# Reordering the last recurrence steps of a fused attention and MLP kernel, and storing the second product's result block by block

## The chip, the core and the metric

The kernel runs on one core of a Trainium2 chip. A core has five engines that work side by side, each with its own instruction queue that it takes in order: TensorE (matmuls, "PE" in the profile, with its weight loads shown as "PEld"), VectorE ("DVE"), ScalarE ("ACT"), GpSimd ("POOL") and SyncE ("SP"). Data comes from and goes to device memory by DMA; in this kernel SP and POOL issue all of these transfers. Matmuls write to PSUM, which has eight banks of 128 x 512 float32 values here; the other engines copy results from there to SBUF.

The metric is the device time of one execution, in microseconds. Smaller is better.

## The reference: what is computed

The first stage is a linear recurrence for each of 4 x 8 batch and head pairs, over 768 tokens with a state of 40 x 40; the second stage is a two-layer network with a Mish activation on the 3072 tokens that result.

```python
def _attn_ref(r, k, v, w, a, b):
    B, H, S, D = r.shape            # 4, 8, 768, 40
    state = np.zeros((B, H, D, D), dtype=np.float32)
    y = np.zeros_like(r)
    for t in range(S):
        ...
        y[:, :, t] = np.einsum('bhd,bhde->bhe', rt, state)
        Sa = np.einsum('bhde,bhe->bhd', state, at)
        state_decay = state * wt[:, :, None, :] - np.einsum('bhd,bhe->bhde', Sa, bt)
        state = state_decay + np.einsum('bhd,bhe->bhde', vt, kt)
    return y

def _moe_ref(x, w_in, w_out):       # x: 3072 x 320, w_in: 320 x 2048, w_out: 2048 x 320
    h = x @ w_in
    sp = np.where(h > 20.0, h, np.log1p(np.exp(np.minimum(h, 20.0))))
    g = h * np.tanh(sp)
    return g @ w_out
```

## The kernel before

**The recurrence.** The 768 tokens are cut into 12 chunks of 64 (`nch` = 12, `C` = 64). A chunk's update is written in closed form, which needs the inverse of a small triangular matrix for each chunk and head. The work on one chunk falls into parts:

- `pre_a` (L126) loads a chunk's inputs (SP queue) and forms its scaled operands. It does not depend on the state.
- `pre_inv` (L205) inverts the triangular blocks of a pair of chunks by forward substitution: a long dependent chain of small VectorE operations (L214, L216), closed by two transposes (L218, L220). There are six pairs, numbered 0 to 5.
- `post_inv` (L223) is the merge of a pair: from the inverted halves it builds the full inverse and from that the operand `KT` of both chunks. For each chunk of the pair it runs two sets of small matmuls (L232, L241) with a ScalarE copy between them (L235), copies pieces into `bdT` on ScalarE (L249 to L251), multiplies (L258) and copies the result into `KT` on ScalarE (L260). The merge of pair 5 serves steps 10 and 11.
- `step` (L349) carries the state through chunk c. It has five parts for each of two groups g of heads, issued in the order of `SORD`: `step_a` (L273: copies the state into `VS`, multiplies with `KT`, L284, and negates the result into `UVT`, L286), `step_u` (L288: transposes, L293, and copies, L294), `step_d` (L296: transposes the state, L304, and copies it, L305), `step_b` (L308: matmuls, L314, and a masked copy on VectorE, L316) and `step_c` (L319: matmuls, L334 and L339, then the new state on VectorE, L342 and L346, and the output `yev` on ScalarE, L343). At its end it issues the loads of the next step (`step_loads`, L265) and the stores of its own y (L370), all on the POOL queue. Each step needs the state of the one before.

The y of every step goes to a buffer in device memory, from which the second stage reads it.

**The dense stage.** `Mlp.run` (L550) works on 6 blocks of 512 tokens. `load_x` (L558) loads a block's y and a scale on the SP queue, multiplies them on VectorE (L567) and splits the product into a high part (L568) and a low rest (L569, L570). `mlp1` (L573), called for q = 0 to 7 in each block, forms 2 x 128 of the 2048 hidden columns: 16 matmuls (L584), Mish on ScalarE (L586), and a split into a high part `gh` (L589) and a rest `gl` (L590). `mlp2` (L595), which follows `mlp1` by three calls, adds the q-th share of the second product: 24 matmuls of 320 columns (L604 to L606) into four PSUM tiles `po`, one for each 128 tokens. At q = 7 the four are copied to SBUF tiles `os` by ScalarE (L610) and stored by SP (L611).

The weights arrive as 64-bit values and are converted on the chip: `load_f32` (L445) loads a chunk on the SP queue (L453), and ScalarE and VectorE turn it into float32 (L459 to L463); `split` (L489) then makes a high part (L494) and a rest (L495). `first` (L527) converts what is left of w_in once the `pre_a` buffers are free; `second` (L532) converts three chunks of w_out and opens the buffers of the dense stage that reuse room of the merge; `third` (L545) converts the other five.

**What sets the order.** The program is written as straight-line Python. A scheduler walks it at compile time and fixes the order of each engine's queue: it takes an instruction by its place in the program, as soon as what it needs is there by the scheduler's own reckoning. The helper `at(tc, k)` (L44) moves all that is issued inside it forward by `OFF[k]` places (backward if the number is negative); two nested calls move by both. In the main loop (L392 on) the end of the program stands in this order: step 8; the inversion and the merge of pair 5 (`inv(5)`, keys I5, I and J5); `first` (key W, 600); step 9; `second` (key V, 400); step 10; step 11; and then the dense stage. In a step every part has a key of its own besides the step's (`c0` 600, `u1` 250, `d0` 250, `d1` 150).

Of the kernel before, what the change touches and what calls it, by code (L numbers as in the profile page):

```python
# [7 lines left out]
F32 = mybir.dt.float32  # L8
# [28 lines left out]

OFF = {'I': 80, 'T1': 80, 'P00': -40, 'P10': 80, 'P11': 40, 'b0': 15, 'c0': 600, 'u0': -15, 'u1': 250, 'd0': 250,
       'd1': 150, 'W': 600, 'V': 400, 'E': 150, 'I0': 600, 'I1': 300, 'I2': 300, 'I3': 300, 'I4': 300, 'p4': 15,
       'I5': 300, 'J5': 600, 's0': 150, 's2': -15, 's3': 80, 's4': 250, 's6': -15, 's7': -40, 's8': 150, 's10': -150}  # L40
SORD = 'a0 b0 u0 d0 a1 b1 u1 d1 c0 c1'


# [423 lines left out]
def load_yp(nc, i, yD, pD, y, p, dup):  # L467
    ys = yD[i].rearrange("b e a (g t) -> (b e a g) t", g=2)
    ps = pD[i].rearrange("b e a (g s t) -> (b e a g) s t", g=2, t=65)[:, :, 0:64]
    p = p.rearrange("p k (s t) -> p k s t", t=64)  # L470
    for k in range(2):
        nc.sync.dma_start(out=y[:, k], in_=ys[k * 128:k * 128 + 128])
        nc.sync.dma_start(out=p[:, k], in_=ps[k * 128:k * 128 + 128])
    for k in range(2 if dup else 1):
        nc.sync.dma_start(out=y[k * 64:k * 64 + 64, 2], in_=ys[256:320])
        nc.sync.dma_start(out=p[k * 64:k * 64 + 64, 2], in_=ps[256:320])


class Mlp:
# [70 lines left out]
    def run(self, nsc):  # L550
        tc, nc, W, yD, pD, out = self.tc, self.tc.nc, self, self.yD, self.pD, self.out
        V, A, PE, SP, G = nc.vector, nc.scalar, nc.tensor, nc.sync, nc.gpsimd
        T = 512
        ps_h, mpa = self.ps_h, self.mpa
        mp = self.pool("mp", 2, "left")
        ps_o = self.pool("ps_o", 8 - NH, "left", space=PSUM)

        def load_x(i):  # L558
            y = self.mpx.tile([128, 3, T], F32, name="xy", bufs=NXP)
            p = self.mpx.tile([128, 3, T], F32, name="xp", bufs=NXP)  # L560
            for c in range(2):
                t = slice(c * 256, c * 256 + 256)
                load_yp(nc, 2 * i + c, yD, pD, y[:, :, t], p[:, :, t], True)

            xh = self.mpx.tile([128, 3, T], F32R, name="xh", bufs=NX)
            xl = self.mpx.tile([128, 2, T], F32R, name="xl", bufs=NX)
            V.tensor_tensor(out=y, in0=y, in1=p, op=ALU.mult)  # L567
            A.copy(xh, y)  # L568
            V.tensor_tensor(out=xl, in0=y[:, 0:2], in1=xh[:, 0:2].bitcast(F32), op=ALU.subtract)  # L569
            V.tensor_tensor(out=xh[64:128, 2], in0=y[64:128, 2], in1=xh[64:128, 2].bitcast(F32), op=ALU.subtract)  # L570
            return xh, xl

        def mlp1(q, xh, xl):  # L573

            g = mpa.tile([128, 2, T], F32, name="g", bufs=NHB)
            for j in range(2):
                ph = ps_h.tile([128, T], F32, name="ph")
                f = slice((q % 2 * 2 + j) * 128, (q % 2 * 2 + j) * 128 + 128)
                h, l = W.ih[q // 2], W.il[q // 2]

                for n, (w, x) in enumerate(((h[:, 0, f], xh[:, 0]), (h[:, 0, f], xl[:, 0]), (h[:, 1, f], xh[:, 1]),
                                            (h[:, 1, f], xl[:, 1]), (l[:, 0, f], xh[:, 0]), (l[:, 1, f], xh[:, 1]),
                                            (h[:, 2, f], xh[:, 2]), (l[:, 2, f], xh[:, 2]))):
                    PE.matmul(ph, w, x, start=(n == 0), stop=(n == 7), skip_group_check=True)  # L584

                A.activation(g[:, j], ph, AF.Mish)  # L586
            gh = mp.tile([128, 2, T], F32R, name="gh", bufs=NGB)
            gl = mp.tile([128, 2, T], F32R, name="gl", bufs=NGB)
            A.copy(gh, g)  # L589
            V.tensor_tensor(out=gl, in0=g, in1=gh.bitcast(F32), op=ALU.subtract)  # L590
            return gh, gl

        pos = {}

        def mlp2(i, q, gh, gl):  # L595
            if q == 0:
                pos[i] = [ps_o.tile([128, 320], F32, name="po") for _ in range(4)]
            po = pos[i]
            for j in range(2):
                f = q * 2 + j  # L600
                oh, ol = (w[f // 2][:, f % 2 * 320:f % 2 * 320 + 320] for w in (W.oh, W.ol))
                for k in range(4):
                    t = slice(k * 128, k * 128 + 128)
                    PE.matmul(po[k], gh[:, j, t], oh, start=(f == 0), stop=False, skip_group_check=True)  # L604
                    PE.matmul(po[k], gh[:, j, t], ol, start=False, stop=False, skip_group_check=True)  # L605
                    PE.matmul(po[k], gl[:, j, t], oh, start=False, stop=(f == 15), skip_group_check=True)  # L606
            if q == 7:
                for k in range(4):
                    o = mp.tile([128, 320], F32, name="os")
                    A.copy(o, po[k])  # L610
                    SP.dma_start(out=out[i * T + k * 128:i * T + k * 128 + 128], in_=o)  # L611

        wait = []
        x = load_x(0)
        for i in range(nsc // 2):
            for q in range(8):
                wait.append((i, q) + mlp1(q, *x))
                if (i, q) == (0, 0):
                    self.third()
                if q == 3 and i + 1 < nsc // 2:  # L620
                    nx = load_x(i + 1)
                if len(wait) > LAG:
                    mlp2(*wait.pop(0))
            x = nx
        for w in wait:
            mlp2(*w)
# [32 lines left out]
```

## Time and profile before

| | |
|---|---|
| three executions | 826.63, 828.1, 833.62 us (median 828.1) |
| the profiled execution | 823.92 us, of which the span from the first to the last instruction is 821.8 us |
| mean granted TensorE clock in it | 0.953 |
| TensorE busy | 722.7 us (88%) |
| VectorE busy | 458.7 us (56%) |
| ScalarE busy | 428.7 us (52%) |
| GpSimd busy | 103.4 us (13%) |
| read from and written to device memory | 48.79 MB and 11.86 MB |

How to read it: times inside the profile count from the first instruction. "L258" is line 258 of the kernel; `pa<-bdT,HA` means that the tile `pa` is written from `bdT` and `HA`; what stands in square brackets is the time for which the engine was idle just before, and what ended that. A busy TensorE is not one at its peak, since matmuls are pipelined: what counts is the distance from one matmul's start to the next. In the first 100 us TensorE is busy for only 51.18 us, while the first chunks are prepared. From there to 460 us the recurrence runs, with the inversions on VectorE beside it; after that comes the dense stage.

### The profile page before, as it was taken

How to read it: one execution, taken by the hardware profiler on the slowest of the kernel's cores; microseconds unless marked ns; L12 is line 12 of the kernel's file. 1: busy time of each engine (PE TensorE's matmuls, PEld its weight loads, DVE VectorE, ACT ScalarE, POOL GpSimd, SP SyncE). 2: the span in 40 equal slices, each digit the busy share in tenths (PEclk: the TensorE clock that was granted, in tenths of full speed). 3: DMA queues.
4: the chain of work that ended last, by engine and by line, in shares of the span. 5: the costliest groups of instructions: out<-in, count | busy, mean ns of one | idle time of the engine just before them, and what ended most of it. 6: DMA issues, size and time to landing. Idle time of an engine off the chain costs nothing.

```text
span 821.8 us, 17217 instructions
## 1 busy us (share of the span) xinstructions
PE 722.7 (88%) x7048; PEld 644.8 (78%) x7048; DVE 458.7 (56%) x957; ACT 428.7 (52%) x931; POOL 103.4 (13%) x182
## 2 busy tenths in 40 slices
PE   2635798899889889888786899999999999999997
PEld 2524697788778778788676789999999999999997
DVE  6689878749899757988954558311312212111110
ACT  5533556784586867567685555343333333432331
POOL 8100012123223022221102100000000000000000
PEclk9855679999999999999999999999999999999999
DMA  6522224323433134423528755210300100000000
GB/s 169 143 65 81 57 53 96 99 67 97 118 103 76 59 96 105 83 58 111 142 76 207 160 157 135 59 51 1 77 33 0 55 17 1 33 1 1 33 1 32
DMA packets 58206, 61.81 MB, mean 75 GB/s; under 512 B 25536, under 2 KB 48704, under 8 KB 58128
## 3 DMA queue, kind: packets, MB, share of 16 engines
q1 hardware_dynamic: 49296, 40.94, 18.3%
q0 software_dynamic: 8832, 19.79, 10.0%
q8 instruction: 55, 0.90, 0.5%
q14 instruction: 23, 0.19, 0.1%
HBM read 48.79 MB, written 11.86 MB: 74 GB/s over the span
## 4 chain that ended last, share of the span: by engine, by line
PE 52%; ACT 9%; DVE 7%; DMA 3%; issue 2%; SPq 0%; ACTq 0%; DVEq 0%
PE ph L584 21%; PE po L605 7%; PE po L604 7%; PE po L606 7%; PE pa L258 2%; PE pa L186 2%; DMA xp<-pD 1%; DVE tmp L214 1%; DVE XL L216 1%; PE pq L314 1%; ACT bdT L249 1%; PE pu L284 1%; ACT bdT L250 1%; DMA cv_d<-in_wi 1%; ACT KT L260 1%
## 5 line engine op out<-in xcount | busy, mean ns | idle before, releaser
L590 DVE TENSOR_TENSOR gl<-g,gh 128x1024 fp32r<-128x1024 f32 x48 | 58.6, 1224 | 207.5 <-ACT gh L589 207.5
L586 ACT ACTIVATE g<-ph 128x512 f32<-128x512 f32 x96 | 57.3, 598 | 180.5 <-PE ph L584 180.3
L186 PE MATMUL pa<-bk,ad 128*128 128x168 f32 x384 | 85.6, 376 | 42.8 <-DVE bk L170 15.0
L604 PE MATMUL po<-w_oh,gh 128*128 128x320 f32 x384 | 118.3, 308 | 0.0
L605 PE MATMUL po<-w_ol,gh 128*128 128x320 f32 x384 | 118.3, 308 | 0.0
L606 PE MATMUL po<-w_oh,gl 128*128 128x320 f32 x384 | 118.3, 308 | 0.0
L584 PE MATMUL ph<-xh,w_ih 128*128 128x512 f32 x288 | 112.7, 393 | 2.0 <-ACT xh L568 2.0
L186 PEld LDWEIGHTS pa<-bk,ad 128*128 128x128 f32 x384 | 71.5, 235 | 48.2 <-issue 22.8
L584 PE MATMUL ph<-xh,w_il 128*128 128x512 f32 x288 | 97.1, 391 | 0.0
L584 PE MATMUL ph<-xl,w_ih 128*128 128x512 f32 x192 | 75.1, 391 | 0.0
L605 PEld LDWEIGHTS po<-w_ol,gh 128*128 128x128 f32 x384 | 72.1, 188 | 2.2
L604 PEld LDWEIGHTS po<-w_oh,gh 128*128 128x128 f32 x384 | 72.1, 188 | 1.8
L606 PEld LDWEIGHTS po<-w_oh,gl 128*128 128x128 f32 x384 | 72.1, 188 | 0.0
L584 PEld LDWEIGHTS ph<-xh,w_ih 128*128 128x128 f32 x288 | 54.1, 188 | 12.1 <-ACT xh L568 2.2
L584 PEld LDWEIGHTS ph<-xh,w_il 128*128 128x128 f32 x288 | 54.0, 188 | 11.6 <-issue 0.2
L216 DVE TENSOR_TENSOR XL<-XL,tmp 128x30 f32<-128x30 f32 (+9 forms) x180 | 58.7, 326 | 2.4
L214 DVE TENSOR_TENSOR tmp<-XL 128x30 f32<-128x30 f32 (+9 forms) x180 | 58.2, 324 | 2.3
L258 PE MATMUL pa<-bdT,HA 128*104 128x128 f32 x384 | 52.2, 289 | 7.0 <-ACT bdT L251 5.5
L258 PEld LDWEIGHTS pa<-bdT,HA 128*104 128x104 f32 x384 | 46.7, 179 | 11.1 <-ACT bdT L251 7.2
L314 PE MATMUL pq<-bdr,UVT 128*128 128x128 f32 x384 | 53.4, 284 | 0.4 <-ACT UVT L286 0.3
L334 PE MATMUL pq<-UVQ,bkn 128*64 128x104 f32 (+1 forms) x768 | 44.7, 254 | 7.8 <-DVE UVQ L316 5.5
L589 ACT CAST gh<-g 128x1024 fp32r<-128x1024 f32 x48 | 50.1, 1048 | 1.3
(89 smaller groups left out, 1212.6 us busy)
## 6 DMA issues: line engine op xcount, KB each, us to landing
wa<-in_wa SPq DMA_DIRECT2D x48, 162.5 KB
bk<-in_bk SPq DMA_DIRECT2D x48, 160.0 KB
cv_d<-in_wi SPq DMA_DIRECT2D x12, 512.0 KB
cv_d<-in_wo SPq DMA_DIRECT2D x8, 640.0 KB
pD<-P POOLq DMA_DIRECT2D x48, 81.2 KB, 2.2
VS<-in_vN POOLq DMA_DIRECT2D x24, 160.0 KB, 3.4
UVT<-in_vD POOLq DMA_DIRECT2D x24, 160.0 KB, 3.9
bdr<-in_rD POOLq DMA_DIRECT2D x24, 160.0 KB, 4.4
```

The lines of the kernel that those rows point to most:

```text
L186: PE.matmul(pt[:, j], ad[:, s0 + j].rearrange("p k a t -> p (k a t)"), bk[:, s0 + j], start=(j == 0), stop=True, skip_group_check=True)
L214: V.tensor_tensor(out=tv, in0=X[:, i + 1:32, i:i + 1].broadcast_to([128, 31 - i, i]), in1=X[:, i:i + 1, 0:i].broadcast_to([128, 31 - i, i] ...
L216: V.tensor_tensor(out=X[:, i + 1:32, 0:i], in0=X[:, i + 1:32, 0:i], in1=tv, op=ALU.add)
L258: PE.matmul(pk[:, j], ha[:, s0 + j], bd[:, s0 + j].rearrange("p a t -> p (a t)"), start=(j == 0), stop=True, skip_group_check=True)
L314: PE.matmul(pq[:, s], UVT[:, g * 4 + s, be * 128:be * 128 + 128], br[:, be, g * 4 + s].rearrange("p a t -> p (a t)"), start=(s == 0), stop ...
L584: PE.matmul(ph, w, x, start=(n == 0), stop=(n == 7), skip_group_check=True)
L586: A.activation(g[:, j], ph, AF.Mish)
L589: A.copy(gh, g)
L590: V.tensor_tensor(out=gl, in0=g, in1=gh.bitcast(F32), op=ALU.subtract)
L604: PE.matmul(po[k], gh[:, j, t], oh, start=(f == 0), stop=False, skip_group_check=True)
L605: PE.matmul(po[k], gh[:, j, t], ol, start=False, stop=False, skip_group_check=True)
L606: PE.matmul(po[k], gl[:, j, t], oh, start=False, stop=(f == 15), skip_group_check=True)
```

## The change

Two things are changed. In the table of offsets the merge of pair 5 loses its 600 places (key J5), step 9 gets 300 (it had none), step 10 gets 150 instead of -150, and step 11 gets 150 (it had none). In `mlp2` the loop over the four 128-token blocks becomes the outer one and the loop over the two hidden slices the inner one; at q = 7 a block is copied and stored right after its own matmuls, where before all four followed the last matmul, and the tile `os` has four buffers instead of two. No instruction is added or removed.

```diff
 OFF = {...
-       'I5': 300, 'J5': 600, 's0': 150, 's2': -15, 's3': 80, 's4': 250, 's6': -15, 's7': -40, 's8': 150, 's10': -150}
+       'I5': 300, 's9': 300, 's11': 150, 's0': 150, 's2': -15, 's3': 80, 's4': 250, 's6': -15, 's7': -40, 's8': 150, 's10': 150}
...
             po = pos[i]
-            for j in range(2):
-                f = q * 2 + j
-                oh, ol = (w[f // 2][:, f % 2 * 320:f % 2 * 320 + 320] for w in (W.oh, W.ol))
-                for k in range(4):
-                    t = slice(k * 128, k * 128 + 128)
+            for k in range(4):
+                t = slice(k * 128, k * 128 + 128)
+                for j in range(2):
+                    f = q * 2 + j
+                    oh, ol = (w[f // 2][:, f % 2 * 320:f % 2 * 320 + 320] for w in (W.oh, W.ol))
                     PE.matmul(po[k], gh[:, j, t], oh, start=(f == 0), stop=False, skip_group_check=True)
                     PE.matmul(po[k], gh[:, j, t], ol, start=False, stop=False, skip_group_check=True)
                     PE.matmul(po[k], gl[:, j, t], oh, start=False, stop=(f == 15), skip_group_check=True)
-            if q == 7:
-                for k in range(4):
-                    o = mp.tile([128, 320], F32, name="os")
+                if q == 7:
+                    o = mp.tile([128, 320], F32, name="os", bufs=4)
                     A.copy(o, po[k])
                     SP.dma_start(out=out[i * T + k * 128:i * T + k * 128 + 128], in_=o)
```

## What is expected of it

> **What bounds the kernel now.** I read the profile's page first, then the busy times by stretch, then the chain of waits in the second half, and last the timelines of TensorE, ScalarE, VectorE and SP between 370 and 480 us and of everything after 815 us.
>
> ```profile
> span 821.8 us, 17217 instructions
> PE   2635798899889889888786899999999999999997
> 400.00:460.65 60.65, 46.94 (x798) 40.58 (x797) 36.02 (x70) 39.95 (x84) 9.04 (x13) 1.00 0.56 136
> 600.00:700.00 100.00, 100.00 (x560) 90.96 (x559) 22.57 (x19) 35.88 (x49) 0.00 (x0) 1.00 0.06 18
> 490.72 3.65 PE ph L584 x16
> 494.38 0.15 PE po L604
> 497.90 3.65 PE ph L584 x16
> ```
>
> The span's own time is 821.8 us. In the stretch rows the first figure after the length is TensorE's busy time, the last three are granted clock, DMA share and GB/s. The row of tenths (20.5 us each) has a 9 in every slice from 472 us to the one before the last: from there on TensorE has no gap that counts, as in the stretch from 600 to 700. One unit of dense work (16 matmuls of the first product, 24 of the second) repeats from 490.72 to 497.90, so 7.18 us. There are 6 blocks of 512 tokens with 8 units each: 48 x 7.18 = 344.6 us. Nothing in the change removes a matmul from these. What can move is what stands before and behind them. Between 400 us and the first dense matmul TensorE is busy 46.94 of 60.65 us, so 13.7 us are idle.
>
> ```profile
> 460.65 1.56 PE L584 MATMUL ph<-xh,w_ih 128*128 128x512 f32 x4 [1.97 <-ACT xh L568]
> 816.60 0.31 PE L606 MATMUL po<-w_oh,gl 128*128 128x320 f32 x1
> ```
>
> The first dense matmul starts at 460.65 and the last ends at 816.91: 356.26 us, of which 344.6 is dense work. The rest, R = 11.7 us, is attention work that TensorE still does after 460.65. So span = T (start of the first dense matmul) + R + 344.6 + tail, with a tail of 821.8 - 816.91 = 4.9 us. The change can act on T, R and the tail.
>
> **The tail: block by block through four buffers.**
>
> ```profile
> 815.28 0.31 PE L606 MATMUL po<-w_oh,gl 128*128 128x320 f32 x1
> 815.63 0.86 ACT L610 COPY os<-po 128x320 f32<-128x320 f32 x2 [11.08 <-PE po L606]
> 817.98 0.91 ACT L610 COPY os<-po 128x320 f32<-128x320 f32 x2 [1.48 <-DMA out<-os]
> ```
>
> Today block 0's last matmul starts at 815.28 and its copy 0.35 us later. Copies 3 and 4 wait 1.48 us for an output DMA, because there are two buffers; copying ends at 818.89, 2.9 us before the span's end. With four buffers and the block outermost, a block's six matmuls end 6 x 3.52/24 = 0.88 us before the next block's. A copy takes 0.43 us, so three copies hide and only the last is left. It starts 0.35 us after the last matmul's start, at 816.95 against 818.46 for today's fourth copy (half of the 0.91 pair behind 817.98). The tail shrinks by 1.5 us to 3.4. The queues behind the copies are ScalarE's and SP's; both are empty there. At the five earlier block ends the same DMA wait goes, worth nothing: TensorE is at 100.00 of 100.00 us across them, and the next unit covers the copies. Cover gone, it would be 5 x 1.48 = 7.4 us; I see no sign of that. The new order issues the same loads and matmuls; its only other effect could be six instead of three in a row into one PSUM bank. The first product puts eight in a row: 3.65/16 = 228 ns for 512 columns against 3.52/24 = 147 ns for 320, 0.42 ns per column and the same 11 ns beside it. So 0; the bounds are plus and minus those 11 ns per matmul, and since eight in a row show no more than three, I keep 0 at both ends.
>
> **The steps and the merge.** Counted from the loops, the merge (post_inv) issues 194 instructions, the conversion of w_in 63, a step 156. Before, the last merge is put 600 places forward. After, it keeps its place, step 9 goes 300 forward: it follows the merge's start by 194 + 63 = 257 places, so its beginning now precedes the whole merge. Step 10 follows the merge's start by 257 + 156 + 21 = 434; 150 forward leaves it behind the merge's 194. So the order becomes step 9, merge, step 10, step 11; step 10 from -150 to +150 and step 11 from 0 to +150 change little more, since the dense work stands behind them both ways. The loads that a step issues for the next one, and the stores of its y, carry no offset, but leave on POOL as soon as their buffers are free, so they move with the steps.
>
> ```profile
> 374.51 1.12 PE L284 MATMUL pu<-KT,VS 104*64 104x64 f32 x16
> 395.07 0.49 DVE L346 TENSOR_TENSOR ST<-stn,R 128x320 f32<-128x320 f32 x1
> 401.01 1.15 PE L284 MATMUL pu<-KT,VS 104*64 104x64 f32 x32
> 423.13 0.83 PE L314 MATMUL pq<-bdr,UVT 128*128 128x128 f32 x6
> 424.51 1.07 ACT L260 COPY KT<-pa 104x512 f32<-104x512 f32 x2
> 430.82 3.79 PE L258 MATMUL pa<-bdT,HA 128*104 128x128 f32 x32 [0.45 <-ACT bdT L251]
> 434.82 0.28 PE L284 MATMUL pu<-KT,VS 104*64 104x64 f32 x2
> 436.46 0.48 DVE L346 TENSOR_TENSOR ST<-stn,R 128x320 f32<-128x320 f32 x1
> ```
>
> Step 8, beside the second half of the merge before, runs from 374.51 to its last state at 395.56: 21 us. Step 9 runs from 401.01 to 436.94: 36 us, with the merge's products (L258) ahead of its own at 430.82 and its L314 pushed to 423.13. KT of step 10 is complete at 425.58, yet step 10 starts at 434.82: it waits 9.2 us for step 9. That is the upper bound of what step 10 can gain. Against it, the merge now gives way:
>
> ```profile
> L343 ACT COPY yev<-pq 128x256 f32<-128x256 f32 x4 | 1.5, 375 | 0.5 <-DVE stn L342 0.5
> L305 ACT COPY smd<-pu 128x512 f32<-128x512 f32 x1 | 0.6, 585 | 0.0
> 410.50:435.50 25.00, 22.12 (x453) 19.21 (x453) 12.27 (x22) 20.66 (x47) 1.48 (x3) 1.00 0.28 79
> ```
>
> ScalarE is busy 20.66 of 25.00 us there, the fourth figure of the stretch row, and the merge's copies are most of it. Step 9's own copies in that stretch, 1.5 + 0.6 = 2.1 us, now go first, so KT of step 10 comes about 2.1 us later. Estimate: step 10 starts 9.2 - 2.1 = 7.1 us earlier, at 427.7; bounds 0 (the merge lost all that step 9 won) and 9.2. I take 7.1, nearer the rows: only these copies are named as passing the merge.
>
> **The first x.** T needs x, whose loads stand on SP behind the w_in conversion and behind one w_out chunk.
>
> ```profile
> 403.10 0.69 ACT L459 ACTIVATE cv_m<-cv_d 128x512 f32<-128x512 f32 x1 [0.30 <-DMA cv_d<-in_wi]
> 409.60 0.67 ACT L459 ACTIVATE cv_m<-cv_d 128x512 f32<-128x512 f32 x1 [0.34 <-DMA cv_d<-in_wi]
> 417.99 0.70 ACT L459 ACTIVATE cv_m<-cv_d 128x512 f32<-128x512 f32 x1
> 426.89 0.68 ACT L459 ACTIVATE cv_m<-cv_d 128x512 f32<-128x512 f32 x1
> 433.85 0.67 ACT L459 ACTIVATE cv_m<-cv_d 128x512 f32<-128x512 f32 x1 [0.41 <-DMA cv_d<-in_wi]
> 434.70 0.33 SPq L453 DMA_DIRECT2D cv_d<-in_wo  x1
> 437.95 0.33 SPq L472 DMA_DIRECT2D xy<-yD  x1
> SPq L453 <- PE pa L258: 4.8, 1, 4.8
> ```
>
> The chunks are 6.5 us apart (403.10 to 409.60), then 8.4 and 8.9 beside the merge's copies, then 7.0. At 7.0 throughout, the conversion ends 8.4 + 8.9 - 14.0 = 3.3 us earlier. But SP holds the w_out chunk until the merge's last L258 (4.8 us of waiting), and all of x is queued behind it. If that L258 ends 2.1 us later, at 436.7, x starts near 437.3: 0.6 us earlier. So between 0.6 and 3.3; I take the middle, 2.0: T = 458.65. Bounds for the range: 2.1 us late, 3.3 early.
>
> **R and the sum.**
>
> ```profile
> 465.26 0.60 ACT L286 ACTIVATE UVT<-pu 128x512 f32<-128x512 f32 x1 [0.98 <-PE pu L284]
> 470.28 3.95 PE L314 MATMUL pq<-bdr,UVT 128*128 128x128 f32 x32
> 478.43 0.61 PE L339 MATMUL pq<-bdr,smd 128*64 128x128 f32 x8
> ```
>
> Moved 7.1 us forward, the steps stand at 458.65 where they stood at 465.75: step 11's last UVT just made. What is left then is L314 to L339, 470.28 to 479.04, less three dense matmuls among them (about 0.9): R = 7.9. Span = 458.65 + 7.9 + 344.6 + 3.4 = 814.5, against 821.8: 7.3 us less. An error in T alone costs little, since R shrinks as T waits. The executions shown have a median of 828.1, the profiled one took 823.92, 4.2 below. I take the difference from the median: 828.1 - 7.3 = **820.8 us**, 0.9% faster.
>
> **Two rules weighed.**
>
> ```profile
> 460.00:462.00 2.00, 1.35 (x4) 0.75 (x4) 1.37 (x2) 1.98 (x4) 1.52 (x2) 0.82 0.79 149
> 462.00:464.00 2.00, 2.00 (x15) 1.42 (x16) 1.90 (x4) 0.80 (x3) 1.08 (x2) 0.50 1.07 182
> 464.00:466.00 2.00, 2.00 (x32) 1.80 (x29) 0.70 (x1) 1.00 (x3) 0.00 (x0) 0.83 1.22 164
> 437.00:457.30 20.30, 14.45 (x198) 12.37 (x199) 10.45 (x18) 10.19 (x21) 3.99 (x7) 1.00 1.03 225
> bdr<-in_rD POOLq DMA_DIRECT2D x24, 160.0 KB, 4.4
> yD<-yev POOLq DMA_DIRECT2D x24, 160.0 KB, 3.9
> ```
>
> The granted clock falls to 0.82, 0.50, 0.83 in three stretches behind the last gaps; lost are 2 x (0.18 + 0.50 + 0.17) = 1.7 us. I leave it in neither sum.
>
> The Trainium skill, "TensorE: Matmul & The Clock Gate", section "Part 1: The HAM clock gate", says that an idle window of about 3.4 us halves the clock until a busy one has passed. By that rule a change that closes the gaps would gain up to 1.7 us more, and one that leaves TensorE waiting for x would keep the loss; the rows here agree in size, 3.4 us at half speed.
>
> The DMA engines are full (share 1.03) at 225 GB/s from 437.00 to 457.30, while x loads.
>
> The Trainium skill, "DMA: Bandwidth & Descriptors", section "Issuing engines are not separate DMA queues", says that transfers issued from different engines run on the same 16 DMA engines and interleave; it speaks against moving step transfers into that stretch, and is the third rival below.
>
> **The rivals.**
> 1. The steps finish before x arrives (R near 0): 458.65 + 344.6 + 3.4 = 806.6, 15.2 less, or 13.5 with a 1.7 us cold start: 812.9 to 814.6 us. For: step 9 may gain 15 us over today (36 against 21). Against: step 10 needs the merge.
> 2. Slower: the merge runs only once step 9 is done. If its end comes 10 us late, the w_out chunk and x behind it start at about 445.5 instead of 437.95, T = 468.6 less 0.4 for the queue = 468.2; step 10 starts where it did or later, R = 7.9; span 824.1, with the cold clock up to 1.7 more, 2.3 to 4.0 worse: 830.4 to 832.1 us. It decides once T + R passes today's 472.35 plus the tail's 1.5, so T = 465.95, a merge some 8 us late; over 1% worse needs T = 474.25, or 472.55 with the cold clock, a merge 14 to 16 us late.
> 3. Shared DMA engines: step 11's r load and step 10's y store (four of 160 KB, 640 KB) fall into x's stretch; at 225 GB/s they cost 2.8 us. T = 461.45, and with R = 7.9 span 817.3: 823.6 us. Against: the same transfers of one step earlier leave the stretch.
> 4. Nothing but the tail: KT comes late by as much as step 9 wins: 828.1 - 1.5 = 826.6 us.
>
> **How the numbers follow.** Under about 1% (8.3 us) a measurement of this kernel can't tell a difference. Forecast 0.45, its own range 817 to 823.6 (step 10's gain 9.2 with the clock's 1.7, down to a gain of 4), 0.23 of it beyond 1%. Rival 1: 0.17, faster. Rival 2: 0.15, of it 0.08 slower by over 1%, 0.07 within. Rival 3: 0.11 and rival 4: 0.12, both within. Faster 0.40, same 0.52, slower 0.08. The range goes from 813 (rival 1) to 829, past no change; rival 2 beyond that and the far end of rival 1 are what it leaves out.
>
> **What would show it.** In the changed profile: the last copy starts 0.35 us after the last matmul's start and no output DMA is waited for (tail). Step 9's last state well before 436.94, near 422 to 426, with KT of step 10 near 427.7 and step 10's first L284 right behind it. The w_out chunk's issue near the merge's last L258, x's first load between 434.6 and 437.4. The first dense matmul at about 458.7, then R near 7.9. It is wrong if step 10 starts after 434, if x's loads start after 438, or if gaps appear on TensorE after the first dense matmul.

## The result, and the profile after

| | before | after |
|---|---|---|
| median of 18 runs each | 826.75 us (821.49 to 833.62) | 834.14 us (830.57 to 839.96) |
| ratio of after to before, 95% interval | | 1.0106 (1.0081 to 1.0131) |
| the profiled execution, its span | 823.92, 821.8 us | 832.43, 830.6 us |

The changed kernel is about 1% slower; the prediction said 0.9% faster. In the terms of the prediction, the profiled spans differ by 8.8 us: T is 20.08 later (460.65 to 480.73), the stretch from there to the end of the last matmul is 9.71 shorter (356.26 to 346.55), and the tail is 1.57 shorter (4.89 to 3.32).

TensorE around the last attention work, from the timeline of the changed kernel (start, length, engine, line, tiles):

```profile
425.32 1.20 PE L241 MATMUL pa<-X,GP 32*32 32x32 f32 x64 [1.04 <-ACT X L235]
...
431.47 1.12 PE L284 MATMUL pu<-KT,VS 104*64 104x64 f32 x16
...
451.04 0.61 PE L339 MATMUL pq<-bdr,smd 128*64 128x128 f32 x8
451.57 1.20 PE L241 MATMUL pa<-X,GP 32*32 32x32 f32 x64
...
458.90 1.56 PE L258 MATMUL pa<-bdT,HA 128*104 128x128 f32 x12
...
469.43 0.61 PE L339 MATMUL pq<-bdr,smd 128*64 128x128 f32 x8
480.73 1.22 PE L584 MATMUL ph<-xh,w_ih 128*128 128x512 f32 x2 [10.69 <-ACT xh L568]
```

The merge works in two halves, one for each chunk of the pair. Its first half (L241 at 425.32) makes `KT` of step 10, which begins at 431.47. Its second half (L241 at 451.57) stands behind the last matmul of step 10 (L339 at 451.04), so its last L258 ends at 460.46; before, that was at 434.61. After step 11's last matmul TensorE has nothing to do for 10.69 us. The operand of that L241 had long been there:

```profile
443.34 0.57 ACT L235 COPY X<-pa 64x512 f32<-64x512 f32 x1
```

`X` was complete at 443.91, and its products waited 7.66 us behind those of step 10. It was the queue's order that held them.

What SP waited for, from its timeline, its waits (in all, times, longest) and VectorE's timeline:

```profile
431.08 0.33 SPq L453 DMA_DIRECT2D cv_d<-in_wi  x1
460.55 0.33 SPq L453 DMA_DIRECT2D cv_d<-in_wo  x1
460.97 0.38 SPq L472 DMA_DIRECT2D xy<-yD  x1
SPq L453 <- PE pa L258: 29.1, 1, 29.1
440.73 0.68 DVE L495 SCALAR_TENSOR_TENSOR w_il<-cv_w,w_ih 128x512 fp32r<-128x512 f32 x1
```

The conversion of w_in ends at 441.41. The w_out chunk and behind it x leave at 460.55 and 460.97, right after the merge's last L258: 29.1 us of waiting in one piece, where before there were 4.8.

The last state of step 8, of step 9 and of step 10 (L346), and the tail (last matmul, then the four copies):

```profile
398.64 0.48 DVE L346 TENSOR_TENSOR ST<-stn,R 128x320 f32<-128x320 f32 x1
424.14 0.49 DVE L346 TENSOR_TENSOR ST<-stn,R 128x320 f32<-128x320 f32 x1
452.05 0.49 DVE L346 TENSOR_TENSOR ST<-stn,R 128x320 f32<-128x320 f32 x1
...
826.97 0.31 PE L606 MATMUL po<-w_oh,gl 128*128 128x320 f32 x1
824.68 0.42 ACT L609 COPY os<-po 128x320 f32<-128x320 f32 x1 [9.76 <-PE po L606]
825.56 0.42 ACT L609 COPY os<-po 128x320 f32<-128x320 f32 x1 [0.46 <-PE po L606]
826.44 0.42 ACT L609 COPY os<-po 128x320 f32<-128x320 f32 x1 [0.46 <-PE po L606]
827.32 0.42 ACT L609 COPY os<-po 128x320 f32<-128x320 f32 x1 [0.46 <-PE po L606]
```

The steps did become faster: step 9's last state stands at 424.63 instead of 436.94, step 10's at 452.54 instead of 459.84. In the tail every copy now waits only for its own block's matmuls; the wait for the output DMA is gone.

**A common zero.** Step 8's last state falls at 395.56 before and at 399.12 after, though both kernels issue the same instructions in the same order up to there. In the profiled executions below it lies anywhere from 393.24 to 410.18. So the experiments are compared in us counted from that point, the span's end too. The ratios use fast runs alone, and the profiled executions of e5, e7 and e8 are slow ones (more than 1.5% above the fastest run of their kernel): of these three only the order of the work and the distances from the common zero are read. The table is worked out from the timelines: a time in the profile less that of step 8's last state. "KT, 2nd half" is the end of the merge's last L258, "w_in" the end of its conversion, "x" the first load of x, "T" the first dense matmul, "last att." the end of the last attention matmul.

```
kernel              step 9  step 10  KT, 2nd half  w_in     x      T   last att.  span's end
before                41.4     64.3          39.1  42.4  42.4   65.1        83.5       426.2
after                 25.5     53.4          61.3  42.3  61.9   81.6        70.9       431.5
e1_offsets            25.9     54.7          62.6  43.6  63.2   83.0        72.2       435.4
e2_queue              27.3     53.6          63.1  42.5  63.2   80.8        72.6       431.3
e3_room               26.1     54.9          62.8  43.7  43.8   64.9        76.0       422.7
e4_s10_back           25.2     61.6          45.0  41.1  45.5   67.5        81.8       425.8
e5_tail               41.3     65.0          39.4  42.3  42.3   65.4        82.4       423.7
e6_tail_room          40.9     64.5          39.0  41.9  41.9   64.6        81.6       422.9
e7_merge_first        41.8     67.9          38.2  42.4  42.4   67.9        85.2       428.2
e8_merge_first_room   41.1     64.3          37.4  41.7  41.8   64.2        82.3       425.4
e9_room_again         26.1     54.7          62.6  43.6  43.6   64.8        75.4       422.0
e10_tail_room_again   42.0     65.2          40.0  43.0  43.0   65.9        82.8       424.0
e11_s10_room          26.2     65.1          46.5  42.7  42.7   65.1        80.7       423.3
e12_room_queue        25.6     54.5          62.4  43.4  43.4   64.6        73.5       423.1
```

Counted so, the change delays the merge's second half by 22.2 us, x by 19.5 and T by 16.5, and finishes the attention work 12.6 us earlier, which nothing uses: from there TensorE waits for x.

### The profile page after: what moved, and what is told of

Read it like the earlier page. It is cut to its first block, busy times and chain, and to the rows that moved or that the text cites. A ratio compares the mean times of both kernels' runs of the same rounds, so it can differ in the third digit from the quotient of the medians.

```text
span 830.6 us, 17217 instructions
## 1 busy us (share of the span) xinstructions
PE 721.0 (87%) x7048; PEld 645.6 (78%) x7048; DVE 459.2 (55%) x957; ACT 429.1 (52%) x931; POOL 103.2 (12%) x182
## 4 chain that ended last, share of the span: by engine, by line
PE 54%; DVE 8%; ACT 7%; DMA 2%; issue 2%; ACTq 0%; SPq 0%; DVEq 0%
PE ph L584 21%; PE po L605 7%; PE po L606 7%; PE po L604 7%; PE pa L258 3%; PE pq L314 2%; DMA cv_d<-in_wi 2%; PE pa L186 2%; DVE XL L216 1%; DVE tmp L214 1%; PE pu L284 1%; ACT KT L260 1%; DVE UVQ L316 1%; PE pa L202 1%; ACT VS L277 1%
## 5 line engine op out<-in xcount | busy, mean ns | idle before, releaser
L186 PE MATMUL pa<-bk,ad 128*128 128x168 f32 x384 | 81.1, 360 | 47.0 <-DVE bk L170 16.7
L186 PEld LDWEIGHTS pa<-bk,ad 128*128 128x128 f32 x384 | 67.3, 223 | 52.4 <-issue 24.5
L584 PEld LDWEIGHTS ph<-xh,w_ih 128*128 128x128 f32 x288 | 54.5, 190 | 20.8 <-ACT xh L568 10.9
L258 PE MATMUL pa<-bdT,HA 128*104 128x128 f32 x384 | 55.2, 301 | 10.0 <-ACT bdT L251 8.8
L258 PEld LDWEIGHTS pa<-bdT,HA 128*104 128x104 f32 x384 | 49.5, 189 | 13.5 <-ACT bdT L251 10.7
L314 PE MATMUL pq<-bdr,UVT 128*128 128x128 f32 x384 | 55.7, 293 | 1.9 <-ACT UVT L286 1.8
L314 PEld LDWEIGHTS pq<-bdr,UVT 128*128 128x128 f32 x384 | 50.3, 205 | 3.4 <-ACT UVT L286 2.2
```

The lines of the kernel that those rows point to most:

```text
L186: PE.matmul(pt[:, j], ad[:, s0 + j].rearrange("p k a t -> p (k a t)"), bk[:, s0 + j], start=(j == 0), stop=True, skip_group_check=True)
L258: PE.matmul(pk[:, j], ha[:, s0 + j], bd[:, s0 + j].rearrange("p a t -> p (a t)"), start=(j == 0), stop=True, skip_group_check=True)
L314: PE.matmul(pq[:, s], UVT[:, g * 4 + s, be * 128:be * 128 + 128], br[:, be, g * 4 + s].rearrange("p a t -> p (a t)"), start=(s == 0), stop ...
```

## The experiments

Each is an edit of the changed kernel. Ratios are to the kernel before, from runs on the same chip, with 95% intervals.

**Which part costs the time?** e1 has the offsets alone (`mlp2` as before), e5 the new `mlp2` alone.

```diff
 # e5_tail
-       'I5': 300, 's9': 300, 's11': 150, ... 's10': 150}
+       'I5': 300, 'J5': 600, ... 's10': -150}
```

> The offsets of the change alone, the second product as before. Theory (late merge): the whole loss comes from the offsets: the first dense matmul starts near 480.7 us of the span as in the changed kernel (460.65 before), and the tail behind the last matmul stays at 4.9 us, so the span is about 830.6 + 1.6 = 832.2 us, some 1.2% slower than before. Rival (the new loop order of the second product costs something): first dense matmul near 480.7, but the stretch from it to the last matmul shorter than the changed kernel's 346.6 us by more than 1 us, and the time nearer to before.

> The loop order of the second product and the four buffers alone, with the offsets of before. Theory: the last copy starts 0.35 us after the start of the last matmul and the tail from the last matmul to the end of the span is 3.3 us (4.9 before); nothing else moves, so counted from the last state of step 8 the span ends at 426.2 - 1.6 = 424.6 us; time 0.2% below before, inside the noise. Rival (the loop order costs TensorE something): from the first dense matmul to the last more than 357.5 us (356.3 before).

e1: 1.0118 (1.0055 to 1.0182), from four runs only. e5: 0.9991 (0.996 to 1.0022). The loss belongs to the offsets. On the clock of the profile e1's first dense matmul (485.50) and its span (837.9) come 5 to 6 us later than expected, of which 3.4 us lie ahead of step 8's last state; from the common zero T is at 83.0 against 81.6. The tail in e5:

```profile
824.98 0.31 PE L606 MATMUL po<-w_oh,gl 128*128 128x320 f32 x1
825.32 0.43 ACT L609 COPY os<-po 128x320 f32<-128x320 f32 x1 [0.45 <-PE po L606]
```

The last copy begins 0.34 us after the last matmul's start, and 3.41 us lie behind the last matmul's end instead of 4.89. That 1.5 us is 0.2%, less than the interval can show.

**What does x wait for?** Two things tie it to the merge. In SP's queue the w_out chunk stands ahead of it, whose buffers reuse room of the merge. And the program's memory map puts x's own load tiles there too: `xy` and `xp` take bytes 147424 to 159712 of each partition, in the room of the pool `iw`, which holds the merge's operands (`HA`, eight buffers in bytes 129408 to 156032). The four of them that this merge reads lie at 132736 to 146048, next to x's tiles and not under them; in the program as built x's first load waits for the last reader of the whole pool all the same. e2 takes all w_out chunks out of x's way; e3 gives `xy` and `xp` a pool opened before `mpx`, which puts them at 167904 to 180192, clear of `iw`.

```diff
 # e2_queue
-NO1 = 3
+NO1 = 0
 # e3_room
+        self.mpy = self.pool("mpy", 1)
         self.mpx = self.pool("mpx", 2)
...
-            y = self.mpx.tile([128, 3, T], F32, name="xy", bufs=NXP)
-            p = self.mpx.tile([128, 3, T], F32, name="xp", bufs=NXP)
+            y = self.mpy.tile([128, 3, T], F32, name="xy", bufs=NXP)
+            p = self.mpy.tile([128, 3, T], F32, name="xp", bufs=NXP)
```

> The changed kernel, with all eight w_out chunks converted in the third conversion stage, so that no w_out chunk stands in front of x's loads on SP. Theory (room): x's buffers lie in the room of the merge's operands HA, so the first x load still waits for the merge's last L258 near 460.5 us and starts within 1 us of it; first dense matmul 478 to 481, span 828 to 832. Rival (queue): x waits only for the w_out chunk in front of it; then its first load starts when w_in's conversion ends, near 441.5, first dense matmul near 461, span near 461 + 9 + 344.6 + 3.3 = 818.

> The changed kernel, with the two tiles that x is loaded into (xy, xp) in a pool of their own, opened first, so that they lie where the w_in conversion was and no longer in the room of HA; the w_out chunks stay in their stage, though x's loads then come out ahead of the first of them on SP. Theory (room): first x load near 441.5 us, right behind the last w_in conversion, first dense matmul near 461, attention work left after it 8 to 10 us, span near 818 (815 to 821), faster than before by about 0.5%. Rival (the loads themselves are slow, or something else holds the first dense matmul): first x load early, but first dense matmul still after 470, span above 825.

SP in e2, timeline and waits, and TensorE's first dense matmul:

```profile
457.11 0.33 SPq L472 DMA_DIRECT2D xy<-yD  x1
SPq L472 <- PE pa L258: 20.6, 1, 20.6
474.73 1.22 PE L584 MATMUL ph<-xh,w_ih 128*128 128x512 f32 x2 [8.17 <-ACT xh L568]
```

With nothing ahead of it in the queue, x itself (L472) now waits 20.6 us for the merge's L258. (On the clock of the profile T and the span of e2 come 3 us short of what was expected, with step 8's last state 5 us earlier, at 393.94.) Ratio 1.0065 (1.0038 to 1.0092): emptying the queue alone does not free x, since its room holds it by itself. The same in e3, with the last attention matmul:

```profile
437.00 0.33 SPq L472 DMA_DIRECT2D xy<-yD  x1
SPq L472 <- DVE w_il L495: 7.5, 1, 7.5
458.19 0.96 PE L585 MATMUL ph<-xh,w_ih 128*128 128x512 f32 x3 [0.81 <-ACT xh L569]
468.62 0.61 PE L339 MATMUL pq<-bdr,smd 128*64 128x128 f32 x8
```

x now waits for the conversion of w_in alone. In the table T goes from 81.6 back to 64.9, while the merge's second half still ends at 62.8. Ratio 0.9926 (0.9882 to 0.9969). So a late merge costs time only through what x is tied to. In e3 the scheduler also put the w_out chunk behind the first loads of x, so both ties are cut in it; whether the queue alone would hold x as long was not tried.

**Which offset delays the merge?** e4 sets step 10 back to -150 and step 11 to 0; e7 keeps all new offsets of the steps, and gives the merge its 600 places again.

```diff
 # e4_s10_back
-       'I5': 300, 's9': 300, 's11': 150, ... 's10': 150}
+       'I5': 300, 's9': 300, ... 's10': -150}
 # e7_merge_first
-       'I5': 300, 's9': 300, 's11': 150, ...
+       'I5': 300, 's9': 300, 's11': 150, 'J5': 600, ...
```

> The changed kernel with step 10 back at -150 and step 11 at 0; step 9 keeps its 300 and the merge has no priority. Theory: step 10's 150 is what puts it ahead of the merge's second half; without it the merge's last L258 ends near 440 to 447 instead of 460.5, the first dense matmul starts near 462 to 468, with 8 to 11 us of attention work left, span 818 to 826. Rival (the loss comes from taking the 600 from the merge, whatever step 10 does): last L258 after 455, first dense matmul after 475, span above 828.

> The changed kernel with the 600 places given back to the merge; steps 9, 10 and 11 keep their new offsets. Theory: the merge's last L258 ends 38 to 43 us after the last state of step 8 (39.1 before, 61.3 in the changed kernel), x's loads start 42 to 44 us after it, the first dense matmul 64 to 67 us, attention work after it 9 to 12 us: span 423 to 427 us after the last state of step 8, time within 0.5% of before. Rival (the offsets of the steps alone push the merge back): last L258 later than 50 us, time over 0.5% above before.

The second half's L258 and the first dense matmul of e4; then step 9's last state and the first dense matmul of e7:

```profile
443.00 3.71 PE L258 MATMUL pa<-bdT,HA 128*104 128x128 f32 x32
469.25 2.07 PE L584 MATMUL ph<-xh,w_ih 128*128 128x512 f32 x4 [3.39 <-ACT xh L568]
...
446.60 0.49 DVE L346 TENSOR_TENSOR ST<-stn,R 128x320 f32<-128x320 f32 x1
473.21 1.20 PE L584 MATMUL ph<-xh,w_ih 128*128 128x512 f32 x4 [1.44 <-ACT xh L568]
```

e4: the second half ends at 45.0 in the table instead of 61.3, so 16 of the 22 us come from the offsets of steps 10 and 11 (the two went back together; in programs built with only one of them set back, which were not run, step 10's -150 puts the second half ahead of step 10's parts c again, and step 11's 0 leaves it behind them). The other 6 remain from step 9 and the lost 600. T is at 67.5, and the ratio 1.0021 (0.9982 to 1.006). e7: the merge ends at 38.2, but step 9 is at 41.8 again, as before the change; ratio 0.9989 (0.9948 to 1.003). So with the merge ahead the steps' new offsets bring nothing that shows, and step 9's 300 lets it go first only where J5 is gone. J5's loss alone does not do it either: in a program built without step 9's 300, which was not run, step 9's parts c end behind both halves of the merge. In e7's profile T and the span's end lie about 1 us past the ranges expected (64 to 67 and 423 to 427), of which the ratio shows nothing.

**What is the steps' order worth once x has its room?** e6 and e10 are the same kernel: e5 with the room of e3. e9 is e3 again, e8 is e7 with the room, e11 is e4 with it, e12 is e2 with it.

> As the last one, and x's two load tiles moved out of the room of HA. Theory (room matters only where the merge is late): with the offsets of before the merge's last L258 ends some 39 us after the last state of step 8 and w_in's conversion some 42 us after it, so x is held by the conversion in any case and its first load stays within 1 us of the conversion's end; the span ends 423.5 to 425.5 us after the last state of step 8, the time within 0.4% of the tail alone. Rival (the room alone is what made the kernel with the moved tiles faster): the span ends at 422.5 or earlier, as there (422.65), so that the offsets bring nothing.

> As the last one, and x's two load tiles moved out of the room of HA. Theory: with the merge first the room frees nothing that the conversion does not hold, so the result stays within 0.4% of the last one; against the changed kernel with the moved tiles (422.65 us after the last state of step 8) it tells what the late merge itself is worth once x no longer hangs on it: if that order is better for the steps, this one is 1 to 3 us slower than it. Rival: this one is as fast or faster, so the whole gain comes from x.

> The kernel of e3 once more (x's tiles in a pool of their own, the changed order of steps), now on the same chip and beside the room with the old order. Theory (the steps' order is worth something once x no longer hangs on the merge): aligned to step 8's last state, the first x load is again at 43 to 45 us, the first dense matmul at 64 to 66 and the last attention matmul at 75 to 77, and the time is 3 to 6 us below before and 2 to 5 us below e10. Rival (the time of e3 was a fortunate chip): the time is within 2 us of before and of e10.

> The kernel of e6 once more (x's tiles in a pool of their own, the old order of steps, the new tail). Both theories: aligned to step 8's last state, x's first load at 42 us, the first dense matmul at 64 to 66, the last attention matmul at 81 to 83; the time is 0 to 2 us below before. If it comes as low as e9, the late steps' order is worth nothing.

> The order of e4 (step 9 forward, step 10 back at -150, step 11 at 0, the merge without its 600 places) with x's tiles in a pool of their own. Theory: the merge ends at 44 to 46 us after step 8's last state as in e4, but x no longer waits for it: its first load at 42 to 44, the first dense matmul at 64 to 66, the last attention matmul at 80 to 82; time between e10 and e9, 1 to 3 us below before. Rival (what e4 lost was not x's room): the first dense matmul at 67 or later, time as e4, 1 to 3 us above before.

> The kernel of e9 with all chunks of w_out converted late (the first three too), so that none can stand ahead of x. Theory (with its own room x waits for nothing but the conversion of w_in): the first x load at 42 to 44 us after step 8's last state, the first dense matmul at 64 to 66, the time within 2 us of e9. Rival (the queue still matters once the room is there): the first dense matmul 2 us or more ahead of e9's, and the time 2 us or more below it.

```
e6   0.9984 (0.9951 to 1.0017)      e10  1.0013 (0.9987 to 1.0038)
e8   0.9992 (0.9950 to 1.0034)      e11  0.9987 (0.9949 to 1.0025)
e9   0.9974 (0.9945 to 1.0004)      e12  1.0007 (0.9978 to 1.0036)
```

The first dense matmul and the last attention matmul in e9, and x's first load and the first dense matmul in e11:

```profile
464.53 0.96 PE L585 MATMUL ph<-xh,w_ih 128*128 128x512 f32 x3 [0.81 <-ACT xh L569]
474.53 0.61 PE L339 MATMUL pq<-bdr,smd 128*64 128x128 f32 x8
...
448.42 0.33 SPq L472 DMA_DIRECT2D xy<-yD  x1
470.82 1.20 PE L585 MATMUL ph<-xh,w_ih 128*128 128x512 f32 x4 [1.61 <-ACT xh L569]
```

With the room, T comes at 64 to 66 whatever the steps' order: x hangs on the conversion of w_in, at 42 to 44 in all of them. That holds for e12 as well, where emptying the queue brings no further gain. In e11 T is 65.1 against 67.5 in e4, so what e4 still lost was the wait of x (45.5 against 42.7). What the order can then win is attention work that no longer stands behind T: the span's end is at 422.0, 422.7 and 423.1 in e9, e3 and e12, at 422.9 and 424.0 in e6 and e10. That is about 1 us on average, no more than e6 and e10, one kernel, differ; 2 to 5 were expected between e9 and e10. (e6 ends 0.6 us below the range that its theory gave.) The times do not settle it: e3's 0.7% shrank to 0.3% in e9, whose interval reaches past 1 and whose medians lie the other way (828.95 us against 828.49 before), and e12, nearly the same kernel, shows none. By its medians e9 is within 2 us of before and of e10 (830.24), which is what its rival said. That the kernel of e3 and e9 beats the one before thus rests on e3's runs alone; it is not settled.

**What stays open.** The table gives the change 5.3 us (431.5 less 426.2) and e1 9.2; the medians of after and before differ by 7.4, the interval of the ratio stands for 6.7 to 10.8 us. One profiled execution of each does not fix the size more closely.

## Why the prediction was wrong

- **Tail: right.** Said was 1.5 us less, with the last copy 0.35 us behind the last matmul's start; measured were 1.57 us and 0.35.
- **Interior blocks and loop order at 0: right.** From T to the end of the last matmul e5 takes 354.80 us, before 356.26: the new loop order costs nothing that shows.
- **Order of the steps: the step that failed.** The prediction counted places, "step 10 follows the merge's start by 434; 150 forward leaves it behind the merge's 194", and made the order "step 9, merge, step 10, step 11". What came is step 9, the merge's first half, step 10, its second half, step 11. The count took a step and the merge for one block each, and it took counted places for the order. The parts of a step carry offsets of their own (600 for `c0`, 250 for `u1` and `d0`, 150 for `d1`). `c0` begins 88 places into the step, and 434 + 88 - 150 - 600 is negative: it is asked for ahead of the whole merge. That is not the whole account, for `c1` carries no offset and came ahead of the second half too, and in a program built with these four offsets at 0 (not run) the second half's L258 still stand behind all of step 10's parts c. The scheduler also goes by what it reckons to be ready; how that led to this order stays open. That the offsets of the last two steps are needed for it, beside J5's loss, is shown by e4.
- **What held step 10 before: misread.** "It waits 9.2 us for step 9" does not hold, since step 10's first L284 (434.82) comes before step 9's last state (436.94). It needs the state of the first group of heads only, and that was in `VS` by 429.41:

```profile
428.48 0.93 ACT L277 COPY VS<-ST 40x320 f32<-40x320 f32 x2
```

After that the second half of the merge (L258 from 430.82 to 434.61) stood ahead of it in TensorE's queue. So step 10 and the second half already competed before; the change turned their order round. Nor was 9.2 us the upper bound: step 10's last state comes 10.9 us earlier (53.4 against 64.3).

- **Step 9 and the start of step 10: the numbers came, in part by luck.** Step 9's last state was to fall between 422 and 426 (424.63). It gained 15.9 us (25.5 against 41.4), about the 15 that rival 1 named. Counted from step 8's last state, step 10's first L284 comes at 32.35 instead of 39.26, 6.9 us earlier, where 7.1 was said. But that is only half of the first group's products; the other half waits for `KT` until 36.97. That the merge loses only 2.1 us to step 9 was mis-sized even for its first half: `KT` of step 10 is complete at 436.53 (two last copies of L260), 37.4 after step 8's last state; before it was 30.0.

```profile
435.46 1.07 ACT L260 COPY KT<-pa 104x512 f32<-104x512 f32 x2
436.09 0.69 PE L284 MATMUL pu<-KT,VS 104*64 104x64 f32 x16 [0.92 <-ACT KT L260]
```

- **x and T: the mechanism right, its size wrong.** SP did hold the w_out chunk until the merge's last L258 (460.46, issue 460.55). But that L258 was put 2.1 us later and came 22.2 later from the common zero (25.9 on the clock of the profile), and T, put 2.0 us earlier, came 16.5 later. The prediction also saw only the queue; that x's own tiles lie in the room of the merge's pool (e2, e3) was missed. It changes no number here, but it would have led to a wrong remedy.
- **The earlier conversion: wrong.** 3.3 us were hoped for at best; the table has 42.4 before and 42.3 after. Part of the second half's copies no longer runs beside it (L251 and L260), but L249 and L250 still do (433.80 to 439.23), and it does not speed up.
- **R.** Said 7.9; no attention work is left behind T, as in rival 1: step 11 ended 11 us ahead of it. It is what kept the loss at 1%.
- **The rivals.** What came is rival 2's late merge with rival 1's early steps. Rival 2 named the mechanism and priced it for a merge 10 us late and R = 7.9; it did not consider that the merge could fall behind step 10 as well. It had 0.15, and slower by over 1% had 0.08: too little for an order that had only been counted.
- **The clock.** Priced at up to 1.7 us if TensorE waits for x; from T to the last matmul's end it took 346.55 us instead of 344.6, so 1.95. The changed kernel's stretches there (the clock is the last column but two):

```profile
480.00:482.00 2.00, 1.23 (x3) 0.51 (x3) 1.26 (x2) 2.00 (x3) 0.00 (x0) 0.50 1.00 389
482.00:484.00 2.00, 2.00 (x5) 1.61 (x6) 1.97 (x4) 1.16 (x3) 0.00 (x0) 0.50 0.29 68
484.00:486.00 2.00, 2.00 (x9) 1.61 (x8) 2.00 (x4) 1.83 (x3) 0.00 (x0) 0.83 0.75 205
```

The Trainium skill, "TensorE: Matmul & The Clock Gate", section "Part 1: The HAM clock gate", says that the array's clock is throttled by default and only sustained activity releases it; after the idle 10.69 us the trace agrees, with 0.50 until 484.

- **Shared DMA engines (rival 3): its condition did not come.** Step 11's loads of r and step 10's stores of y were issued at 452.80 and 454.48, ahead of x's first load at 460.97. From there to the first dense matmul x took 19.8 us (460.97 to 480.73) against 22.7 before (437.95 to 460.65), where a step's loads ran beside it (POOL, 441.59 and 448.31); that these made the difference is argued, not shown. Nor were 225 GB/s the most that the DMA engines move, as the price took it. While TensorE stood idle they moved 284 GB/s:

```profile
470.65:480.73 10.08, 0.00 (x0) 0.00 (x0) 4.66 (x6) 3.03 (x4) 1.00 (x2) 0.69 0.85 284
```

## What to carry to other kernels

Before work is moved past other work, list for each piece what is released when it ends, room in SBUF included: here half a merge, which only the last step needed, held the memory into which the next stage loads, and finishing the steps 12.6 us earlier could not pay for that. Where a scheduler works from offsets, counted places do not give the order; the order of the queues is fixed when the program is built, and can be read there before a run. When a transfer waits, test its queue and its destination apart, as the one can hide the other: with the queue emptied, x waited for the same matmul.

## What was not expected of the hardware

The same instructions in the same order take different times up to step 8's last state: 393.24 us in e3, 410.18 in e12, a spread of 17 us, about twice what the change costs. The two ran on different chips, but e9 (399.75) and e12, on one chip, still differ by 10 us. The states, and one stretch ahead of them, in e3 and then in e12:

```profile
392.76 0.48 DVE L346 TENSOR_TENSOR ST<-stn,R 128x320 f32<-128x320 f32 x1
200.00:300.00 100.00, 87.72 (x1321) 77.36 (x1319) 83.86 (x205) 71.50 (x187) 21.12 (x40) 0.98 0.33 89
...
409.69 0.49 DVE L346 TENSOR_TENSOR ST<-stn,R 128x320 f32<-128x320 f32 x1
200.00:300.00 100.00, 89.11 (x1226) 79.84 (x1224) 84.34 (x218) 64.76 (x174) 21.10 (x38) 0.91 0.31 86
```

The granted clock in that stretch is 0.98 in the one and 0.91 in the other, with TensorE busy for 88 and 89 of 100 us: it issues 1321 matmuls in the one and 1226 in the other. What makes the clock differ while the work is the same was not found. It means that two profiled executions can only be compared from a point that both have reached with the same work.
